# Decode step with modulation: the output projection's weights in one load, and the result turned through a bf16 PSUM tile

## The chip, the cores and the metric

The kernel runs on one core of one Trainium2 chip. Times are device microseconds (us) of whole executions, as medians of several runs. Profile times are microseconds from the start of the profiled execution's span, which is about 1.3 us shorter than its timed duration (420.02 against 418.7 us).

## The reference

One decode step of a modulated transformer block for two sequences: attention with 32 query heads over 4 key/value heads and 32768 cached positions, a projection `wo`, then a two-layer network. Cut to what matters here:

```python
mod = (silu(c) @ w_mod)                       # 6 vectors of 1024 for each sequence
h = layernorm(x) * (1 + ca) + sa
q = h @ wq                                    # 1024 -> 32 heads of 128
p = softmax(q @ k_cache.T * 128 ** -0.5)      # caches: 2 x 4 x 32768 x 128, bf16
o = p @ v_cache
x = x + ga * (o.reshape(B, 1, 4096) @ wo)     # wo: 4096 x 1024, 8 MB
h = layernorm(x) * (1 + cb) + sb
x = x + gb * (gelu(layernorm(h) @ w1 + b1) @ w2 + b2)   # w1, w2: 7.3 MB each
return x                                      # 2 x 1 x 1024, bf16
```

## The kernel before

All large inputs are streamed through a ring of 160 KB per partition. A list `stream` holds the loads in order; each has a place in the ring, and SyncE issues the next one when everything that had used that place has been read. The order of issue is fixed, so one load that has to wait holds up all behind it.

```python
def add_k(i, hf):   # K of round i in two halves of 32 KB to a partition
    add(("K", i, hf), [2, TPC * D], ..., hf * 32 * KB, f"K{hf}")      # places 0 and 32
def add_v(i):       # V of round i, 64 KB to a partition
    add(("V", i), [NCH, TPC * D], ..., 64 * KB, "V")                  # place 64
# ... w_mod, then wq (places 96 and 128), then K, K, V of the 8 rounds, then:
for m, off in enumerate((128, 0)):
    add(("wo", m), [16, DM], A_wo[m * 2048:(m + 1) * 2048, :].rearrange("(p j) n -> p j n", j=16), off * KB)
for m, off in enumerate((32, 64)):
    add(("w1", m), [4, F], w1_v[:, 4 * m:4 * m + 4, :], off * KB)
for m, (j0, j1, off) in enumerate(W2_ITEMS):  # 8, 8, 8, 3 and 1 rows of w2
    add(("w2", m), [j1 - j0, DM], w2_v[:, j0:j1, :], off * KB)
```

A round transposes K on the PE, multiplies it with q, takes the softmax and multiplies with V. At its end the head outputs are rescaled, picked out of a 128x128 product and put into `atT`, the transposed operand of the `wo` product:

```python
dve(... scalar_tensor_tensor(out=pick[:, :, :], in0=psM[:, 256:384] ..., scalar=rinv[:, 0:1], in1=m8 ...))
dve(... tensor_reduce(at[:, :], pick.rearrange("p e j -> p j e"), AX.X, ALU.add))
lo = 64 * (g % 2)
T.inst("pool", lambda e: e.tensor_copy(atT[g // 2][lo:lo + 64, :, b], at[lo:lo + 64, :]), ...)
```

After the rounds come the loads of two biases, the `wo` product (64 matmuls on four column groups of the PE), two layernorms, the `w1` product, gelu, the `w2` product (32 matmuls into rows for its first 16 rows, 96 into columns for the last 12), and the turn of the result:

```python
for m in range(2):
    it = need("wo", m)
    for j in range(16):
        for hf in range(2):
            q = 2 * (j % 2) + hf
            pe(... matmul(psS[0][32 * q:32 * q + 32, :], lhsT=atT[m][:, j, :], rhs=w[:, j, hf * 512:(hf + 1) * 512], ...))
# ... layernorm, w1, gelu, w2 ...
pe(... matmul(psM[0:16, 0:128], lhsT=res_bf.rearrange("p b k -> p (b k)"), rhs=ident[:, :], start=True, stop=True))
dve(lambda e: e.tensor_copy(res16[:, :], psM[0:16, 0:128]), ...)     # psM is float32
```

## Time and profile before

| | before |
|---|---|
| median, three runs | 420.02 us (419.86 to 420.03) |
| span of the profile | 418.7 us |
| bytes loaded, mean rate over the span | 178.42 MB, 426 GB/s |
| last bytes of the stream | before 415.5 us |
| PE, VectorE, ScalarE busy | 70%, 50%, 36% |

The profile is read from two sides. The busy rows show which resource never rests (the DMA engines). The timeline of the last 90 us shows each group of instructions with its start, its length and, in brackets, how long its engine had stood idle and what ended that. A group whose bracket names a DMA waited for bytes; a group whose bracket names an engine waited for computing. The lines themselves are in the prediction.

### The profile page before, as it was taken

The numbers are of one execution on the slowest core, as the hardware profiler recorded it, in microseconds if no ns is written. First come the engines' busy times: TensorE is split into PE (matmuls) and PEld (weight loads), VectorE is DVE, ScalarE is ACT, GpSimd is POOL, SyncE is SP. The second block draws the span as 40 slices with busy tenths as digits, with TensorE's granted clock in tenths as the row PEclk, the third lists the DMA queues.
The fourth block names the chain that finished last, engine by engine and source line by source line (L and its number), as shares of the span: only waits on it lengthen the run. The fifth ranks groups of instructions, "written<-read, shape, count | busy, mean of one in ns | idle before, by whom it ended". The sixth has DMA issues, their size and how long they took to land.

```text
span 418.7 us, 11609 instructions
## 1 busy us (share of the span) xinstructions
PE 291.0 (70%) x5183; PEld 231.3 (55%) x5183; DVE 209.6 (50%) x423; ACT 149.4 (36%) x179; POOL 6.8 (2%) x29
## 2 busy tenths in 40 slices
PE   1407449766996895699369957976995699564536
PEld 1104219762993794299149926962894399221214
DVE  1201105546677676467726664766477567620411
ACT  2000015533565364256405632643365166400100
POOL 3000000000000000000000000000000000000000
PEclk9999557986896997799589958986697889576585
DMA  9989999999999999999999999999999999899995
GB/s 373 450 380 449 448 404 493 398 406 446 441 432 429 423 451 429 419 454 457 391 435 476 407 416 448 438 438 426 438 438 426 416 460 457 377 448 428 424 427 249
DMA packets 5581, 178.42 MB, mean 426 GB/s; under 512 B 698, under 2 KB 706, under 8 KB 964
## 3 DMA queue, kind: packets, MB, share of 16 engines
q1 hardware_dynamic: 5572, 178.28, 98.8%
q8 instruction: 8, 0.13, 0.1%
q14 instruction: 1, 0.01, 0.0%
HBM read 178.28 MB, written 0.00 MB: 426 GB/s over the span
## 4 chain that ended last, share of the span: by engine, by line
DMA 71%; PE 24%; DVE 2%; issue 1%; ACT 1%; SPq 1%
DMA V<-in_A_v_cache_dram 39%; DMA wo<-in_A_wo_dram 10%; DMA K<-in_A_k_cache_dram 10%; PE psZ L584 10%; DMA w<-in_B_w_dram 9%; PE psKT L536 8%; DMA wmod<-in_w_mod_dram 4%; PE psS L548 1%; PE psZ L548 1%; PE psS L655 1%; PE psZ L729 1%; PE psZ L469 1%; ACT KT_sb L540 0%; PE psS L469 0%; DVE m1c L553 0%
## 5 line engine op out<-in xcount | busy, mean ns | idle before, releaser
L536 PE MATMUL psKT<-ident,K 128*128 128x128 bf16 x2048 | 163.1, 229 | 11.5 <-DMA K<-in_A_k_cache_dram 11.5
L540 ACT ACTIVATE KT_sb<-psKT 128x1024 bf16<-128x1024 bf16 x96 | 98.2, 1025 | 124.4 <-PE psKT L536 124.4
L542 DVE COPY KT_sb<-psKT 128x1024 bf16<-128x1024 bf16 x160 | 106.7, 688 | 61.6 <-PE psKT L536 61.2
L536 PEld LDWEIGHTS psKT<-ident,K 128*128 128x128 bf16 x2048 | 126.7, 102 | 13.0 <-DMA K<-in_A_k_cache_dram 12.7
L584 PE MATMUL psZ<-V,E_sb 128*32 128x512 bf16 x512 | 46.4, 541 | 23.2 <-DMA V<-in_A_v_cache_dram 20.0
L548 PE MATMUL psS<-qcur,KT_sb 128*128 128x8 bf16 x1024 | 44.7, 167 | 2.2 <-issue 2.2
L584 PEld LDWEIGHTS psZ<-V,E_sb 128*32 128x32 bf16 x512 | 18.7, 130 | 47.7 <-issue 38.8
L548 PE MATMUL psZ<-qcur,KT_sb 128*128 128x8 bf16 x1024 | 43.0, 167 | 2.2 <-issue 1.5
L548 PEld LDWEIGHTS psS<-qcur,KT_sb 128*128 128x128 bf16 x1024 | 40.0, 97 | 2.3 <-issue 2.3
L548 PEld LDWEIGHTS psZ<-qcur,KT_sb 128*128 128x128 bf16 x1024 | 37.9, 96 | 3.4 <-issue 1.6
L572 ACT ACTIVATE E_sb<-S_sb 128x512 bf16<-128x512 f32 x32 | 19.5, 630 | 29.6 <-DVE S_sb L570 29.6
L570 DVE TENSOR_TENSOR S_sb<-S_sb,gmb 128x512 f32<-128x512 f32 x32 | 20.0, 685 | 0.3
L576 DVE TENSOR_REDUCE rs<-E_sb 128x8 f32<-128x512 bf16 x32 | 19.7, 675 | 0.0
L469 PE MATMUL psS<-wmod,inT 128*32 128x512 bf16 x32 | 5.1, 624 | 16.2 <-DMA wmod<-in_w_mod_dram 16.2
L553 DVE TENSOR_REDUCE m1c<-psZ 128x8 f32<-128x512 f32 x16 | 11.1, 693 | 10.2 <-ACT S_sb L552 10.1
L595 DVE RECIPROCAL rinv<-psM 128x1 f32<-128x1 f32 x8 | 1.3, 168 | 27.7 <-PE psM L593 27.7
L605 PE MATMUL psM<-msum,hmat 128*128 128x128 f32 x16 | 4.2, 347 | 13.3 <-DVE msum L600 13.3
L559 PE MATMUL psM<-identf,m 128*8 128x128 f32 x16 | 4.3, 369 | 13.1 <-DVE m L556 13.1
L553 DVE TENSOR_REDUCE m1c<-psS 128x8 f32<-128x512 f32 x16 | 11.1, 693 | 3.2 <-ACT S_sb L552 3.1
L552 ACT ACTIVATE S_sb<-psZ 128x512 f32<-128x512 f32 x16 | 9.5, 595 | 7.5 <-PE psZ L548 7.5
L477 DVE COPY S_sb<-psS 128x512 f32<-128x512 f32 x1 | 0.7, 690 | 22.9 <-PE psS L469 22.9
L469 PEld LDWEIGHTS psS<-wmod,inT 128*32 128x32 bf16 x32 | 1.1, 132 | 19.3 <-DMA wmod<-in_w_mod_dram 18.0
(123 smaller groups left out, 167.5 us busy)
## 6 DMA issues: line engine op xcount, KB each, us to landing
K<-in_A_k_cache_dram SPq DMA_DIRECT2D x16, 4096.0 KB, 27.1
wq<-in_A_wq_dram SPq DMA_DIRECT2D x2, 4096.0 KB, 44.8
wo<-in_A_wo_dram SPq DMA_DIRECT2D x2, 4096.0 KB, 39.0
w<-in_B_w_dram SPq DMA_DIRECT2D x2, 3584.0 KB, 32.5
wmod<-in_w_mod_dram SPq DMA_DIRECT2D x1, 6144.0 KB, 29.8
w<-in_B_w_dram SPq DMA_DIRECT2D x3, 2048.0 KB, 37.8
wmod<-in_w_mod_dram SPq DMA_DIRECT2D x1, 4608.0 KB, 15.8
wmod<-in_w_mod_dram SPq DMA_DIRECT2D x1, 1536.0 KB, 6.0
```

Of the source, the lines that this page charges most:

```text
L469: pe(lambda e, w=it.view, k=k, kk=kk, ch=ch, n=n, q=q: e.matmul(bank[n][32 * q:32 * q + 32, :], lhsT=inT[:, k, :], rhs=w[:, kk, ch * 512:( ...
L536: pe(lambda e, kq=kq, jj=jj, w=kt, t=t: e.transpose(psKT[kq][:, jj * 128:(jj + 1) * 128], w[:, t, :], ident[:, :]), reads=[it.reg, "ident" ...
L540: act(lambda e, src=src: e.activation(KT_sb[g8][:, :, :], src, ACT.Copy), reads=[f"psKT{kq}"], writes=[f"KT_sb{g8}"], sem=f"ev{cc}_{g8}")
L542: dve(lambda e, src=src: e.tensor_copy(KT_sb[g8][:, :, :], src), reads=[f"psKT{kq}"], writes=[f"KT_sb{g8}"], sem=f"ev{cc}_{g8}")
L548: pe(lambda e, t=t, jj=jj: e.matmul(ps[:, t * HPG:(t + 1) * HPG], lhsT=KT_sb[g8][:, jj, :], rhs=qcur[:, :], start=True, stop=True), reads= ...
L552: act(lambda e: e.activation(Sc, ps.rearrange("p (t h) -> p h t", h=HPG), ACT.Copy), reads=[preg], writes=[f"S_sb_{cc}"], sem=f"sc{cc}")
L553: dve(lambda e: e.tensor_reduce(m1c[:, :, cc], ps.rearrange("p (t h) -> p h t", h=HPG), AX.X, ALU.max), reads=[preg], writes=[f"m1c{cc}"])
L559: pe(lambda e: e.matmul(psM[0:HPG, 0:128], lhsT=m1[:, :], rhs=identf[:, :], start=True, stop=True), reads=["m1", "identf"], writes=["psM"])
L570: dve(lambda e: e.tensor_tensor(Sc, Sc, gmb[:, :].unsqueeze(2).to_broadcast([128, HPG, TPC]), ALU.subtract), reads=[f"S_sb_{cc}", "gmb"], ...
L572: act(lambda e: e.activation(Ec, Sc.rearrange("p h (u t) -> p u h t", t=4), ACT.Exp, scale=SCALE), reads=[f"S_sb_{cc}"], writes=[f"E_sb_{c ...
L576: dve(lambda e: e.tensor_reduce(rs4[:, :, cc], Ec.rearrange("p u h t -> p h u t"), AX.XY, ALU.add), reads=[f"E_sb_{cc}"], writes=[f"rs4_{c ...
L584: pe(lambda e, t4=t4, tg=tg, q=q: e.matmul(psO[32 * q:32 * q + 32, :], lhsT=E_sb[:, tg // 4, :, :].rearrange("p h t -> p (h t)"), rhs=vt[: ...
```

## The change

Its intent: one 8 MB load of `wo`, with 64 contiguous KB to a partition, in place of two of 4 MB with 32 KB, which needs another row layout (a partition holds 32 consecutive rows, so each head group fills a quarter of the partitions and not a half of one of two operands); and a cheaper last step, in which the result is transposed into a bf16 PSUM tile and copied from there. The core of the diff (shapes of the small helpers `hmat`, `rsum16`, `m8`, `pick` change with it, cut here):

```diff
-W2_ITEMS = (..., (16, 24, 128), (24, 27, 144), (27, 28, 150))
+W2_ITEMS = (..., (16, 24, 0), (24, 27, 16), (27, 28, 22))
-    at = sb("at", [128, 16], BF16)
-    atT = [sb(f"atT{i}", [128, 16, 32], BF16) for i in range(G // 2)]
+    at = sb("at", [128, 32], BF16)
+    atT = sb("atT", [128, 32, 32], BF16)
-    for m, off in enumerate((128, 0)):
-        add(("wo", m), [16, DM], A_wo[m * 2048:(m + 1) * 2048, :].rearrange("(p j) n -> p j n", j=16), off * KB)
+    add(("wo", 0), [32, DM], A_wo.rearrange("(p j) n -> p j n", j=32), 0)
-    for m, off in enumerate((32, 64)):
+    for m, off in enumerate((128, 64)):
         add(("w1", m), ...)
-        lo = 64 * (g % 2)
-        ... e.tensor_copy(atT[g // 2][lo:lo + 64, :, b], at[lo:lo + 64, :]) ...
+        lo = 32 * g
+        ... e.tensor_copy(atT[lo:lo + 32, :, b], at[lo:lo + 32, :]) ...
-    for m in range(2):
-        it = need("wo", m)
-        for j in range(16):  ... lhsT=atT[m][:, j, :] ...
+    it = need("wo", 0)
+    for j in range(32):  ... lhsT=atT[:, j, :] ...
-    pe(lambda e: e.matmul(psM[0:16, 0:128], lhsT=res_bf..., rhs=ident[:, :], start=True, stop=True), ...)
-    dve(lambda e: e.tensor_copy(res16[:, :], psM[0:16, 0:128]), ...)
+    pe(lambda e: e.transpose(psKT[0][0:16, 0:128], res_bf..., ident[:, :]), ...)
+    dve(lambda e: e.tensor_copy(res16[:, :], psKT[0][0:16, 0:128]), ...)
```

More of the change, by code (lines that the diff above doesn't have):

```diff
@@ L36 @@
 WMOD_ITEMS = ((0, 1), (1, 4), (4, 8))
-W2_ITEMS = ((0, 8, 96), (8, 16, 112), (16, 24, 128), (24, 27, 144), (27, 28, 150))
+W2_ITEMS = ((0, 8, 96), (8, 16, 112), (16, 24, 0), (24, 27, 16), (27, 28, 22))
 EVAC_PATTERN = ("dve", "act", "dve", "act", "dve", "dve", "act", "dve")
@@ L258, in bass_adaLN_cond__gqa_block_cached__mixer_channel_mlp__decode_kernel @@
     onesf = sb("onesf", [128, 128])
-    hmat = sb("hmat", [128, 2, HPG, 8])
+    hmat = sb("hmat", [128, G, HPG, 4])
     hsel = sb("hsel", [128, HPG])
     mk4 = sb("mk4", [128, 4])
-    m8 = sb("m8", [128, 8])
+    m8 = sb("m8", [128, 4])
     mblk = sb("mblk", [128, KT8])
@@ L265, in bass_adaLN_cond__gqa_block_cached__mixer_channel_mlp__decode_kernel @@
     c16 = sb("c16", [16, 128], BF16)
-    rsum16 = sb("rsum16", [128, 2, HPG, 8])
+    rsum16 = sb("rsum16", [128, G, HPG, 4])
     msum = sb("msum", [128, 128])
@@ L411, in bass_adaLN_cond__gqa_block_cached__mixer_channel_mlp__decode_kernel @@
     T.inst("pool", lambda e: e.memset(onesf[:, :], 1.0), writes=["onesf"])
-    for t, nm in [(inT, "inT"), (gT, "gT")] + [(atT[g], f"atT{g}") for g in range(G // 2)]:
+    for t, nm in ((inT, "inT"), (gT, "gT"), (atT, "atT")):
         T.inst("pool", lambda e, t=t: e.memset(t[:, :, :], 0.0), writes=[nm])
@@ L451, in bass_adaLN_cond__gqa_block_cached__mixer_channel_mlp__decode_kernel @@
     dve(lambda e: e.tensor_reduce(hsel[:, :], identf.rearrange("p (c h t) -> p h c t", c=4, h=HPG), AX.XY, ALU.add), reads=["identf"], writes=["hsel"])
-    dve(lambda e: e.tensor_copy(hmat[:, :, :, :], hsel[:, :].unsqueeze(1).unsqueeze(3).to_broadcast([128, 2, HPG, 8])), reads=["hsel"], writes=["hmat"])
-    dve(lambda e: e.tensor_reduce(m8[:, :], identf.rearrange("p (h e) -> p e h", e=8), AX.X, ALU.add), reads=["identf"], writes=["m8"])
+    dve(lambda e: e.tensor_copy(hmat[:, :, :, :], hsel[:, :].unsqueeze(1).unsqueeze(3).to_broadcast([128, G, HPG, 4])), reads=["hsel"], writes=["hmat"])
+    dve(lambda e: e.tensor_reduce(m8[:, :], identf.rearrange("p (h e) -> p e h", e=4), AX.X, ALU.add), reads=["identf"], writes=["m8"])
     dve(lambda e: e.tensor_reduce(mblk[:, :], identf.rearrange("p (k u) -> p k u", u=16), AX.X, ALU.add), reads=["identf"], writes=["mblk"])
@@ L527, in next_q @@
         b, g = i % 2, i // 2
-        T.inst("pool", lambda e: e.tensor_copy(qcur[:, :], qT[:, b, g * HPG:(g + 1) * HPG]), reads=["qT"] + [f"atT{g}" for g in range(G // 2)], writes=["qcur"], sem="qc")
+        T.inst("pool", lambda e: e.tensor_copy(qcur[:, :], qT[:, b, g * HPG:(g + 1) * HPG]), reads=["qT", "atT"], writes=["qcur"], sem="qc")
     def tr(i, cc, g8):
@@ L591, in row_sums @@
         dve(lambda e: e.tensor_reduce(rowsum[:, :], rs4[:, :, :], AX.X, ALU.add), reads=[f"rs4_{cc}" for cc in range(NCH)], writes=["rowsum"])
-        dve(lambda e: e.tensor_copy(rsum16[:, :, :, :], rowsum[:, :].unsqueeze(1).unsqueeze(3).to_broadcast([128, 2, HPG, 8])), reads=["rowsum"], writes=["rsum16"], sem="rs")
+        dve(lambda e: e.tensor_copy(rsum16[:, :, :, :], rowsum[:, :].unsqueeze(1).unsqueeze(3).to_broadcast([128, G, HPG, 4])), reads=["rowsum"], writes=["rsum16"], sem="rs")
         pe(lambda e: e.matmul(psM[:, 144:145], lhsT=rsum16.rearrange("p g h e -> p (g h e)"), rhs=onesf[:, 0:1], start=True, stop=True),
@@ L606, in extract_2 @@
            reads=["hmat", "msum"], writes=["psM"])
-        dve(lambda e: e.scalar_tensor_tensor(out=pick[:, :, :], in0=psM[:, 256:384].rearrange("p (e j) -> p e j", j=16), scalar=rinv[:, 0:1],
-                                             in1=m8[:, :].unsqueeze(2).to_broadcast([128, 8, 16]), op0=ALU.mult, op1=ALU.mult),
+        dve(lambda e: e.scalar_tensor_tensor(out=pick.rearrange("p e j -> p (e j)").rearrange("p (e j) -> p e j", j=32), in0=psM[:, 256:384].rearrange("p (e j) -> p e j", j=32), scalar=rinv[:, 0:1],
+                                             in1=m8[:, :].unsqueeze(2).to_broadcast([128, 4, 32]), op0=ALU.mult, op1=ALU.mult),
             reads=["psM", "rinv", "m8"], writes=["pick"], sem="pk")
@@ L612, in red @@
             with nc.allow_low_precision("one nonzero term in each sum"):
-                return e.tensor_reduce(at[:, :], pick.rearrange("p e j -> p j e"), AX.X, ALU.add)
+                return e.tensor_reduce(at[:, :], pick.rearrange("p e j -> p (e j)").rearrange("p (e j) -> p j e", j=32), AX.X, ALU.add)
         dve(red, reads=["pick"], writes=["at"])
-        lo = 64 * (g % 2)
-        T.inst("pool", lambda e: e.tensor_copy(atT[g // 2][lo:lo + 64, :, b], at[lo:lo + 64, :]), reads=["at"], writes=[f"atT{g // 2}"], sem="ac")
+        lo = 32 * g
+        T.inst("pool", lambda e: e.tensor_copy(atT[lo:lo + 32, :, b], at[lo:lo + 32, :]), reads=["at"], writes=["atT"], sem="ac")
     rounds = {}
@@ L648, in bass_adaLN_cond__gqa_block_cached__mixer_channel_mlp__decode_kernel @@
     T.dma("sp", lambda e: e.dma_start(b1m[:, :], B_b1.rearrange("(q r) -> q r", r=448)), key="ld_b1", writes=["b1m"])
-    for m in range(2):
-        it = need("wo", m)
-        for j in range(16):
-            for hf in range(2):
-                q = 2 * (j % 2) + hf
-                pe(lambda e, w=it.view, m=m, j=j, hf=hf, q=q: e.matmul(psS[0][32 * q:32 * q + 32, :], lhsT=atT[m][:, j, :], rhs=w[:, j, hf * 512:(hf + 1) * 512],
-                                                                       start=(m == 0 and j < 2), stop=(m == 1 and j >= 14), skip_group_check=True),
-                   reads=[it.reg, f"atT{m}"], writes=["psS0"], mark=(j == 15 and hf == 1))
+    it = need("wo", 0)
+    for j in range(32):
+        for hf in range(2):
+            q = 2 * (j % 2) + hf
+            pe(lambda e, w=it.view, j=j, hf=hf, q=q: e.matmul(psS[0][32 * q:32 * q + 32, :], lhsT=atT[:, j, :], rhs=w[:, j, hf * 512:(hf + 1) * 512],
+                                                              start=(j < 2), stop=(j >= 30), skip_group_check=True),
+               reads=[it.reg, "atT"], writes=["psS0"], mark=(j == 31 and hf == 1))
     def load_row(e_name, b, b_reg, n, parts=128):
@@ L733, in bass_adaLN_cond__gqa_block_cached__mixer_channel_mlp__decode_kernel @@
     dve(lambda e: e.tensor_tensor(res_bf.rearrange("p b k -> p k b"), mT[:, :, :], x1b[:, :, :], ALU.add), reads=["mT", "x1b"], writes=["res_bf"])
-    pe(lambda e: e.matmul(psM[0:16, 0:128], lhsT=res_bf.rearrange("p b k -> p (b k)"), rhs=ident[:, :], start=True, stop=True),
-       reads=["res_bf", "ident"], writes=["psM"])
-    dve(lambda e: e.tensor_copy(res16[:, :], psM[0:16, 0:128]), reads=["psM"], writes=["res16", "c16"])
+    pe(lambda e: e.transpose(psKT[0][0:16, 0:128], res_bf.rearrange("p b k -> p (b k)"), ident[:, :]), reads=["res_bf", "ident"], writes=["psKT0"])
+    dve(lambda e: e.tensor_copy(res16[:, :], psKT[0][0:16, 0:128]), reads=["psKT0"], writes=["res16", "c16"])
     s_out = nc.alloc_semaphore("s_out")
```

## The prediction

> **What bounds the kernel now.** I read the page first: the slices and the chain that ended last.
>
> ```profile
> DMA  9989999999999999999999999999999999899995
> DMA 71%; PE 24%; DVE 2%; issue 1%; ACT 1%; SPq 1%
> ```
>
> The DMA engines are busy from the first slice to the last but one; no compute engine is. The page adds 178.42 MB at a mean of 426 GB/s: 178.42 / 0.426 = 419 us, the whole span (418.7 us). So the kernel is one stream of loads, and a change counts only if it (a) opens a hole in the stream, (b) changes its rate or bytes, or (c) moves the few microseconds after the last load. Next I read the timeline of the last 90 us, where everything the diff touches lies, apart from small work in each round.
>
> ```profile
> 330.98 14.05 SPq L389 DMA_DIRECT2D wo<-in_A_wo_dram  x2
> 355.02 21.65 SPq L389 DMA_DIRECT2D w<-in_B_w_dram  x7
> 362.51 6.34 PE L584 MATMUL psZ<-V,E_sb 128*32 128x512 bf16 x64 [2.93 <-DMA V<-in_A_v_cache_dram]
> 372.10 3.25 PE L655 MATMUL psS<-wo,atT 128*32 128x512 bf16 x32 [0.78 <-DMA wo<-in_A_wo_dram]
> 381.73 3.55 PE L655 MATMUL psS<-wo,atT 128*32 128x512 bf16 x32 [6.39 <-DMA wo<-in_A_wo_dram]
> 385.34 0.69 DVE L664 COPY S_sb<-psS 128x512 f32<-128x512 f32 x1 [13.23 <-PE psS L655]
> 395.75 1.68 PE L696 MATMUL psZ<-w,inT 128*32 128x448 bf16 x16
> 400.59 1.12 DVE L704 STREAM_TRANSPOSE S_sb<-psZ 128x896 f32<-128x896 f32 x1 [2.84 <-PE psZ L696]
> 403.68 1.05 PE L720 MATMUL psS<-w,gT 128*32 128x512 bf16 x16 [3.15 <-DMA w<-in_B_w_dram]
> 408.41 1.90 PE L720 MATMUL psS<-w,gT 128*32 128x512 bf16 x16 [3.69 <-DMA w<-in_B_w_dram]
> 413.27 2.91 PE L729 MATMUL psZ<-gT,w 128*128 128x2 bf16 x96 [0.30 <-DMA w<-in_B_w_dram]
> 417.03 0.28 DVE L736 CAST c<-psM 16x128 bf16<-16x128 f32 x1 [0.37 <-PE psM L734]
> ```
>
> The bracket gives the idle time before a group and what ended it. The last V lands at about 362.4, the first half of wo at about 371.9, the second at 381.65, w1's second half by 398.7, and pieces of w2 at 403.6, 408.4 and 413.2: arrivals set the pace, and the PE waits for each. From wo to w2 there are thus spare microseconds between "computed" and "landed". The first fetch of w, at 355.02, comes when the last K half has been transposed, which frees its buffer; the same moment will release the new wo.
>
> The stretches between landings give the rate (columns: stretch, its length, busy time of the five engines, granted clock, DMA share, GB/s):
>
> ```profile
> 343.00:362.40 19.40, 14.23 (x331) 13.40 (x328) 13.88 (x26) 10.62 (x15) 0.00 (x0) 0.88 0.97 421
> 362.40:371.90 9.50, 7.14 (x68) 3.16 (x68) 4.67 (x13) 1.86 (x2) 0.00 (x0) 0.68 1.02 442
> 371.90:381.65 9.75, 3.25 (x32) 1.09 (x32) 0.20 (x1) 0.00 (x0) 0.25 (x1) 0.68 0.97 420
> ```
>
> The first stretch is (nearly) the last V: 8.39 MB, and 64 KB to a partition, in 19.4 us. The other two are wo, 4.19 MB each and 32 KB to a partition: 9.50 + 9.75 = 19.25 us for the same bytes. The rate depends little, if at all, on whether a partition gets 32 or 64 KB.
>
> **What the Trainium skill says.** (1) "DMA: Bandwidth & Descriptors", Where 436 GB/s comes from: 16 ports of 32 bytes at 850 MHz give 435.2 GB/s. The trace agrees: 434 GB/s over the stretch from 60 to 320 us, 426 over the span. Nothing is left to win in the rate. (2) Same page, Queues, rings and completion order: each DMA engine takes its descriptors in ring order. So wo, issued behind V, starts when V is through, however early it was issued; that agrees with wo landing 41.1 us after its issue at 330.98. (3) "TensorE: Matmul & The Clock Gate", Part 1: the PE starts at half clock and gets the full one after some 3.4 us of activity, in free-running windows. The trace agrees: the second 32 wo matmuls take 3.55 us (111 ns each), with a granted clock of 0.50 from 381.5 to 385.0 and 1.00 from 385.5; w1's last 32 take about 1.8 us (56 ns each). (4) "VectorE: DVE Perf Modes", Why PSUM operands drop a tier: a source in PSUM allows at most the two-fold mode, and float32 there none. The trace agrees: a bf16 PSUM copy of 128x1024 takes 688 ns, a float32 one of 128x512 takes 690 ns.
>
> **The change part by part.**
>
> *One load of 8 MB in place of two of 4.* Same bytes, same place in the queue. One issue less (0.35 us on the SyncE queue, which is not on the path). The old halves were issued at 330.98 (its space was free) and 344.7 (first K half transposed). The new one covers the space of both K halves, so it goes out at 355.02. At that moment the queue still holds the rest of V: 362.4 - 355.0 = 7.4 us of work for the average engine. Is that enough? A hole needs an engine to run dry before the first wo descriptor reaches it. The engines' spread at the end of the stream is an upper guess of their skew: the last microseconds run 352, 246, 197, 86, 0 GB/s in half microseconds from 413.5, so the fastest engine ends some 2 to 2.5 us ahead of the slowest. 7.4 - 2.5 = 4.9 us are left for an issue to reach the engines; the whole out-store, issue to landing, takes 1.4 us. So: no hole, cost 0. wo then lands at 381.7, as its second half does now.
>
> *The order behind it.* w1's first half moves to space free since wq, so its only wait is the queue's order: it follows wo at 355.4 (now 355.02). The second half and the first two pieces of w2 still wait for the last V's matmuls (368.8). The last three w2 pieces wait for the wo matmuls, now over at 375.4, then at about 388. At 388 there is still queued work until w2's second piece lands at 408.4: 20 us. Cost 0.
>
> *The wo matmuls.* Now 32 run at 372.1 under the second half's load, and 32 after 381.7. Afterwards all 64 run after 381.7: the first 32 cold, 3.5 us; the other 32 warm at 56 ns, 1.8 us, or cold, 3.5 us. So the row copy (385.34) and everything that hangs on it is 1.8 to 3.5 us later. Follow that. inT is ready for w1 at 395.75 + 1.8..3.5 = 397.6..399.3. The 64 w1 matmuls took 4.8 us, of which part was a wait for the second half, landed at 398.7. Now they are limited by the PE: at most 38 cold (107 ns) and 26 warm (56 ns) = 5.5 us, so they end at 402.9 to 404.8 instead of 400.55. From there to gT it was 402.74 - 400.55 = 2.2 us: 405.1 to 407.0. The 16 matmuls of w2's first piece (landed 403.6) take 1.05 warm or 1.9 cold: done at 406.2 to 408.6. The second piece lands at 408.4. So the delay ends in the wait for it: cost 0, at the worst corner about 0.2 us, and that meets the 0.3 us between the end of the column turn (412.98) and the landing at 413.2. The spare time, 3.7 us before the second piece, is what pays for it.
>
> *A possible gift.* With the PE working later, its idle gap before 408.4 shrinks from 3.7 us to 0-2 us, so it may still be warm for the end. The 96 last matmuls take 2.91 us at clock 0.50. Warm, they could save up to 0.5 us, no more, since the last piece itself lands only at about 415.4 and 8 matmuls follow. I give that 30%: -0.15 us on average.
>
> *The turn of the result.* The product with the identity into float32 PSUM becomes a transpose into bf16 PSUM: 276 ns as before by my estimate (same 128 columns). The copy reads bf16: by the two rows above, a column costs 690-688 = about the same for twice the columns, so 128 columns fall from 133 to 67 ns above the same 150: 0.28 to 0.21 us. On the path: -0.07 us. Its bank was last used in the rounds, so there is no new wait.
>
> *In each of the 8 rounds.* The pick works on 4 x 32 instead of 8 x 16: still 128 elements, 0.35 + 0.37 us, and a 32x32 GpSimd copy for a 64x16 (0.25 us). All come after the signal that releases the next V load (the row sums' matmul, L593) and before a K transposition that waits for its load. Cost 0.
>
> Sum: 420.02 - 0.07 - 0.15 + about 0.1 for the corners = 419.9 us.
>
> **Rivals.** *A hole in the stream.* The new wo waits for the last transposition, and the queue is down to 7.4 us, less than in any round (14 us of K were still to land when the last V was issued at 329.08). For it: with a late issue an engine that runs far ahead would idle, and DMA idle time is lost for good. Against it: the spread of about 2.5 us. If true, 1 to 5 us: 421 to 425. *The tail becomes compute-bound.* Nothing of wo is worked off before 381.7; if all of it ran cold and w1 too, w2's first piece would be done a microsecond after the second landed. Against it: 3.7 us spare. It would make 420.3 to 421.5. *A gain from fewer, larger packets.* For it: one completion less. Against it: V with 64 KB (421 GB/s) isn't faster than wo with 32 KB (430). If true by 2% over 8 MB, 0.4 us: 419.6. *A loss of rate from 64 KB to a partition:* the same size, the other way: 420.4.
>
> **Range and chances.** The sum is 419.9; a stream of 178 MB repeats within about 0.1 us here (419.86 to 420.03), but another order of loads can land some tenths apart. 8 in 10: 419.2 to 420.9, wider above, for the hole. Two per cent are 8.4 us: no term above comes near, up or down. Faster 0.01, same 0.98, slower 0.01.
>
> **What would show it.** Right: one wo issue at about 355, the DMA busy as before between 350 and 365, the first wo matmul at about 381.7, 64 of them in 5.3 to 7 us, the row copy at 387 to 389, the PE waiting for the second w2 piece at about 408.4 and for the third at 413.2, a last copy of about 0.21 us. Wrong: a dip in DMA share near 358 to 363 and every later landing shifted by it (the hole); no wait before the second w2 piece's matmuls (compute-bound); all landings shifted from wo on without a dip (rate).

## The result, and the profile after

The changed kernel takes 419.93 us (median of six runs, 419.79 to 420.10), the kernel before 420.01 us (six runs, 419.86 to 420.07). The ratio is 0.9999, with a 95% interval from 0.9986 to 1.0011: the same time. Ratios here are the mean time of one kernel's runs over the mean of the other's in the same rounds, so not quite the ratio of the medians quoted. The one above takes in all six runs; those of the experiments leave out each kernel's first run, the profiled one, which the medians and ranges include.

The page of the changed kernel, the row of the DMA engines and the chain that ended last:

```profile
DMA  9989999999999999999899999999999999999996
DMA 73%; PE 26%; SPq 0%; issue 0%; DVE 0%
```

The stream is as full as before. (Line by line the chain now runs through K, 56%, where it ran through V, 39%: wo's issue now hangs on the last K transposition, so the walk back takes that branch. It is another path through the same full stream, not another time.) The timeline of the changed kernel, SyncE's issues first, then the groups that answer to those shown of before:

```profile
353.55 0.35 SPq L388 DMA_DIRECT2D wo<-in_A_wo_dram  x1
353.94 35.77 SPq L388 DMA_DIRECT2D w<-in_B_w_dram  x7
...
362.57 5.21 PE L583 MATMUL psZ<-V,E_sb 128*32 128x512 bf16 x64 [4.46 <-DMA V<-in_A_v_cache_dram]
381.79 5.83 PE L653 MATMUL psS<-wo,atT 128*32 128x512 bf16 x64 [11.54 <-DMA wo<-in_A_wo_dram]
387.68 0.69 DVE L662 COPY S_sb<-psS 128x512 f32<-128x512 f32 x1 [16.64 <-PE psS L653]
398.29 1.68 PE L694 MATMUL psZ<-w,inT 128*32 128x448 bf16 x16
404.15 1.12 DVE L702 STREAM_TRANSPOSE S_sb<-psZ 128x896 f32<-128x896 f32 x1 [3.85 <-PE psZ L694]
406.35 1.55 PE L718 MATMUL psS<-w,gT 128*32 128x512 bf16 x16 [2.27 <-DVE gT L709]
408.46 1.87 PE L718 MATMUL psS<-w,gT 128*32 128x512 bf16 x16 [0.56 <-DMA w<-in_B_w_dram]
413.48 2.84 PE L727 MATMUL psZ<-gT,w 128*128 128x2 bf16 x96 [1.29 <-DMA w<-in_B_w_dram]
417.17 0.21 DVE L733 COPY c<-psKT 16x128 bf16<-16x128 bf16 x1 [0.36 <-PE psKT L732]
```

Three things are to be seen. First, wo goes out 22.6 us later than its first half did (353.55 against 330.98), and its matmuls still start at 381.79, where the second half's started at 381.73. Second, the row copy is 2.3 us later (387.68 against 385.34), w2's first matmuls 2.7 us later (406.35 against 403.68), and the group after that starts within 0.05 us of where it did (408.46 against 408.41): the bracket before it has shrunk from 3.69 to 0.56 us. What was lost came out of a wait. Third, the last copy takes 0.21 us in place of 0.28.

So the times agree because the stream sets the end, and the changed parts either keep their place in the stream or lie in waits for it. Two parts of this can be tried: how much later wo's issue could still be, and how much later the work behind wo.

### The profile page after: what moved, and what is told of

Read it like the earlier page. It is cut to its first block, busy times and chain, and to the rows that moved or that the text cites. A ratio compares the mean times of both kernels' runs of the same rounds, so it can differ in the third digit from the quotient of the medians.

```text
span 418.8 us, 11607 instructions
## 1 busy us (share of the span) xinstructions
PE 284.7 (68%) x5183; PEld 226.4 (54%) x5183; DVE 209.6 (50%) x423; ACT 149.3 (36%) x179; POOL 7.3 (2%) x28
## 4 chain that ended last, share of the span: by engine, by line
DMA 73%; PE 26%; SPq 0%; issue 0%; DVE 0%
DMA K<-in_A_k_cache_dram 56%; PE psKT L535 18%; DMA wo<-in_A_wo_dram 7%; DMA w<-in_B_w_dram 6%; DMA wmod<-in_w_mod_dram 4%; PE psS L547 3%; PE psZ L547 2%; PE psS L653 1%; PE psZ L727 1%; PE psZ L468 1%; PE psS L468 0%; SPq L388 0%; SPq L403 0%; SPq L404 0%; PE psKT L732 0%
## 5 line engine op out<-in xcount | busy, mean ns | idle before, releaser
L535 PE MATMUL psKT<-ident,K 128*128 128x128 bf16 x2048 | 159.8, 226 | 13.2 <-DMA K<-in_A_k_cache_dram 13.2
L535 PEld LDWEIGHTS psKT<-ident,K 128*128 128x128 bf16 x2048 | 123.9, 101 | 14.6 <-DMA K<-in_A_k_cache_dram 14.6
L583 PE MATMUL psZ<-V,E_sb 128*32 128x512 bf16 x512 | 44.8, 526 | 27.0 <-DMA V<-in_A_v_cache_dram 25.4
L653 PE MATMUL psS<-wo,atT 128*32 128x512 bf16 x64 | 5.8, 545 | 11.5 <-DMA wo<-in_A_wo_dram 11.5
```

Of the source, the lines that this page charges most:

```text
L535: pe(lambda e, kq=kq, jj=jj, w=kt, t=t: e.transpose(psKT[kq][:, jj * 128:(jj + 1) * 128], w[:, t, :], ident[:, :]), reads=[it.reg, "ident" ...
L583: pe(lambda e, t4=t4, tg=tg, q=q: e.matmul(psO[32 * q:32 * q + 32, :], lhsT=E_sb[:, tg // 4, :, :].rearrange("p h t -> p (h t)"), rhs=vt[: ...
L653: pe(lambda e, w=it.view, j=j, hf=hf, q=q: e.matmul(psS[0][32 * q:32 * q + 32, :], lhsT=atT[:, j, :], rhs=w[:, j, hf * 512:(hf + 1) * 512] ...
```

## The experiments

Each is an edit of the changed kernel unless it says otherwise; each gave correct results. "Landing" below is taken from the start of the matmuls that waited for the load.

### wo_in_v: wo issued after the last V has been used

```diff
-    add(("wo", 0), [32, DM], ..., 0)
+    add(("wo", 0), [32, DM], ..., 64 * KB)
-    for m, off in enumerate((128, 64)):
+    for m, off in enumerate((128, 0)):
-W2_ITEMS = ((0, 8, 96), (8, 16, 112), (16, 24, 0), (24, 27, 16), (27, 28, 22))
+W2_ITEMS = ((0, 8, 28), (8, 16, 44), (16, 24, 64), (24, 27, 80), (27, 28, 86))
```

> The changed kernel with wo put into the space of V instead of that of the two K halves, so that its load can only be issued after the last V's matmuls (about 368, some 6 us after the last V has landed at 362.5); the other pieces of w1 and w2 go to space that is free earlier. Theory (the kernel is one stream of loads, and the change cost nothing because at the issue of wo, 353.6, 9 us of V were still queued): the stream runs dry, wo and every landing after it come later by 368.1 - 362.4 plus an issue-to-first-data time of 1.5 to 2 us, 7 to 8 us in all: about 427.5 us (426.5 to 428.5). Rival (the late issue of wo doesn't matter, because the end is set by the chain of compute after wo, which has spare time to lose): less than 4 us, under 424.

Measured: 429.48 us (429.07 to 430.62) against 420.19, ratio 1.0232 (1.0215 to 1.0249). The timeline, then the stretches around the hole (columns as in the prediction: length, busy time of the five engines, clock, DMA share, GB/s):

```profile
367.54 0.35 SPq L388 DMA_DIRECT2D wo<-in_A_wo_dram  x1
389.67 5.14 PE L653 MATMUL psS<-wo,atT 128*32 128x512 bf16 x64 [19.71 <-DMA wo<-in_A_wo_dram]
417.42 1.90 PE L718 MATMUL psS<-w,gT 128*32 128x512 bf16 x16 [2.72 <-DMA w<-in_B_w_dram]
```

```profile
357.50:360.00 2.50, 0.41 (x2) 0.31 (x2) 2.02 (x5) 1.13 (x2) 0.00 (x0) 0.50 0.97 419
360.00:362.50 2.50, 0.17 (x4) 0.17 (x8) 2.50 (x6) 2.48 (x4) 0.00 (x0) 0.50 0.02 4
```

The hole is there (the DMA share is 0.02 from 360.0 to 362.5), and it is paid in full, so the rival falls: spare time in the chain behind wo buys nothing for a stream that has run dry. wo lands 7.9 us later than in the changed kernel (389.67 against 381.79), as expected. But the time grew by 9.3 us, over the expected 7 to 8: from wo's landing to that of w2's second piece it took 27.75 us, against 26.67 in the changed kernel. This further 1.1 us was not expected; the next runs meet it again, and wo_wait_m1 shows where it arises.

A remark on reading: the stretch shows almost no bytes after 360.0, yet V's matmuls are released at 362.33. A load is moved in packets, and the kept trace lists each with its start and length. A packet of V or wo has 64 KB and takes 2.42 us; V's last ones start before 360.0 and end between 360.3 and 361.9. So the view books a packet's bytes when it starts. The first packets of wo start 1.0 to 1.8 us after its issue (368.5 to 369.3); the expectation's 1.5 to 2 us for this had no measurement behind it. And these first 16 packets, one on each engine, take 2.6 to 3.4 us in place of 2.42.

### wo_wait_max and wo_wait_m1: wo issued closer to the landing of the last V

```diff
+    T.wait("sp", reads=["gmb"])      # wo_wait_max; reads=["m1"] in wo_wait_m1
     it = need("wo", 0)
```

> The changed kernel, with one more wait before wo's issue: the SyncE queue waits for the last round's broadcast maximum, so wo goes out at about 358.3 instead of 353.6, with 4 us of V still queued for the average engine. Theory (a hole needs an engine to run dry; skew 2 to 2.5 us by the prediction's estimate, issue to first data 1.5 to 2 us): 4.1 - 2.5 - 2 is about zero: 419.9 to 420.5 us, every landing after wo at most 0.5 us later. Rival (the margin of the changed kernel is already nearly used up, the skew is larger): 1.5 to 4 us more, 421.5 to 424.

Measured: 422.08 us (420.92 to 422.40) against 420.19, ratio 1.0038 (1.0021 to 1.0054). The rounds of this profiled run were later on the PE, so wo went out at 360.95 and not at 358.3; the planned dose was missed.

```profile
360.95 0.35 SPq L388 DMA_DIRECT2D wo<-in_A_wo_dram  x1
...
362.83 5.67 PE L583 MATMUL psZ<-V,E_sb 128*32 128x512 bf16 x64 [2.12 <-DMA V<-in_A_v_cache_dram]
382.95 5.85 PE L654 MATMUL psS<-wo,atT 128*32 128x512 bf16 x64 [11.98 <-DMA wo<-in_A_wo_dram]
410.91 1.90 PE L719 MATMUL psS<-w,gT 128*32 128x512 bf16 x16 [1.81 <-DMA w<-in_B_w_dram]
```

wo lands 1.2 us later than in the changed kernel and w2's second piece 2.5 us later: as after the large hole, a further loss arises behind wo (27.96 us between the two, against 26.67). All 16 first packets of wo are slow here too, 2.6 to 3.5 us. The loss of 2.2 us lies in the rival's range, but at a later issue than either side was stated for. The earlier wait was a second dose:

> A second dose of the margin, as the first came out smaller than planned (wo_wait_max issued wo only 1.9 us before the last V landed, and lost 2.2 us). Here the SyncE queue waits for the last round's first maximum, some 2 us earlier: wo goes out about 4 to 6 us before the last V lands at 362.5. Theory (data of a load start 1.0 us after its issue, as in the two runs with a hole, and the engines finish V within 2.4 us of each other, one packet of 64 KB): no engine runs dry, 419.9 to 420.3 us. Rival (the stream needs wo queued long before): over 420.8.

Measured: 421.33 us, scattered from 420.01 to 421.97, against 420.08, ratio 1.0019 (1.0004 to 1.0035). In the profiled run, of 421.97 us:

```profile
358.62 0.35 SPq L388 DMA_DIRECT2D wo<-in_A_wo_dram  x1
...
382.34 5.75 PE L654 MATMUL psS<-wo,atT 128*32 128x512 bf16 x64 [11.94 <-DMA wo<-in_A_wo_dram]
410.49 1.90 PE L719 MATMUL psS<-w,gT 128*32 128x512 bf16 x16 [2.52 <-DMA w<-in_B_w_dram]
```

The expectation was wrong: 3.9 us before V's landing (362.51) is not enough, though one of the four runs lost nothing. Only 0.55 us was lost up to wo; another 1.5 us by w2's second piece (28.15 us from wo's landing, against 26.67). The median of the four, 421.33, is where its rival put it, over 420.8. The end of the stream shows where the loss is: in the last three microseconds with traffic, 415 to 418, it moves 117, 25 and 10 GB/s, where the changed kernel moves 221 and 64 from 414 to 416 and nothing more. 25 GB/s is about what one of 16 engines carries (434 / 16 = 27). So one engine finishes late, and a load counts as landed only with its last engine.

The packets in the trace say how. Five of the 16 first packets of wo take longer than the usual 2.42 us, 2.53 to 3.49 us, and one engine had stood idle for at least 0.6 us before its first. The slowest packet, of 3.49 us, starts at 361.55; followed from packet to packet, its engine ends wo at 381.97, the others by 381.37. At 388.33, six packets of w1 later, one engine moves a packet of 16 KB for another queue, of which the page shows only the sum:

```profile
q8 instruction: 8, 0.13, 0.1%
```

That packet takes 0.93 us, and the w1 packet next to it 1.56 in place of 1.06: 1.4 us in all. The trace doesn't name engines, but the sum says that it is the late one: 381.97 + 16 packets of w1 at 1.06 + 1.41 = 400.34, where w1's second half in fact ends (the other engines by 398.57). w2's second piece then ends at 410.06, on the others by 408.29.

An instruction packet at this place stands in every kept trace, in the changed kernel at 388.41. There the engines end wo at 379.9 to 381.4, and the one that carries this packet is among the first, at 379.93: its lead of 1.5 us hides the 1.4 us. After a late issue of wo the lead is gone and the packet shows. In wo_in_v, where all engines start wo within 0.8 us of each other, the engine with this packet ends 0.9 us behind the rest, most of the further 1.1 us. What remained was why a late issue takes the lead away: why the first packets are slow, and what the small loads in front of wo have to do with it.

### m1_biases_early and finest_biases_early: the small bias loads out of the way

Between the last V and wo lie five loads of biases, 9.0 KB in all (the expectations' 7.9 is a slip: 2 KB of b2 and 7 KB of b1), on 1 to 8 partitions. The Trainium skill, "DMA: Bandwidth & Descriptors", Why a DMA increments its semaphore by 16 and not by 1, says that a load over few partitions runs on as few engines, the lowest-numbered ones. The trace has one packet for each row, 16 in all; no run here shows an engine's number.

```diff
 # against wo_wait_m1; finest_biases_early: the same against w2_finest, without the wait
+    # at the kernel's start, from ScalarE's queue:
+    for r0, r1 in ((0, 1), (1, 3), (3, 7), (7, 8)):
+        T.dma("act", ... b2m[r0:r1, :] ...)
+    T.dma("act", ... b1m ...)
     ...
-    # the same five from SyncE's queue, before wo
```

> wo_wait_m1 with the five small loads of the two biases (7.9 KB in all, a few hundred bytes to a packet) taken from between the last V and wo and issued from ScalarE's queue at the kernel's start. wo_wait_m1 lost 0.0 to 2.0 us although wo was issued 3.9 us ahead of the last V's landing; its stream ends in a taper, 117, 25, 10 GB/s in the last three microseconds, the rate of one engine alone, so one or a few engines lag behind the rest. Theory A (the small loads run one after the other on the few lowest engines, with nothing queued behind them when wo is late, so these engines start wo late; the page on DMA says that few partitions mean few engines): without them the loss is gone, 419.8 to 420.2 us, and no taper. Theory B (the late issue of wo itself makes engines lag): as wo_wait_m1, 420 to 422 us with the same scatter.

Measured: 419.99 us (six runs: four from 419.87 to 420.07, two of 421.52 and 422.76) against 419.98, ratio 1.0018 (0.9997 to 1.0039). Inconclusive. Two runs still lost over a microsecond, so the bias loads are not the whole cause, if any of it. The four good runs can't be credited to them either: in the profiled one wo went out at 357.45, 4.9 us ahead of V's landing (362.33), and not 3.9. In that run no first packet of wo is slow, and the stream ends as in the changed kernel. Against theory A speak the packets of wo_wait_m1: the bias loads take 0.02 or 0.04 us each, 0.5 us in all, far too little for a lag of over a microsecond. For theory B (the late issue itself) speak the slow first packets of wo after each of the later issues. Why they are slow stays open, and so does what the engines did in the runs without a profile.

> w2_finest with the small bias loads at the start likewise: the candidate for a version faster than both kernels. In the changed kernel, too, the stream tapers off: 221 and 64 GB/s in the last two microseconds. Theory A: part of that taper is the lag that the small loads give the lowest engines before wo; without it the last pieces land 0.3 to 1 us earlier, and with pieces this small the end follows them: 419.2 to 419.7 us. Theory B (the taper is the engines' ordinary spread): 419.9 to 420.1.

Measured (w2_finest, below, with the bias loads at the start): 419.90 us (419.78 to 420.32) against 419.98, ratio 0.9995 (0.9982 to 1.0007). Not distinguishable from either kernel; in its profile, of the slowest run, the taper is 270 and 102 GB/s, no shorter than w2_finest's 229 and 80. Theory B fits better.

### w1_ahead: the hole of wo_in_v filled with w1

As wo_in_v, with w1's first half, whose place is free, issued before wo:

```diff
-    add(("wo", 0), [32, DM], ..., 64 * KB)
     for m, off in enumerate((128, 0)):
         add(("w1", m), [4, F], ..., off * KB)
+        if m == 0:
+            add(("wo", 0), [32, DM], ..., 64 * KB)
```

> As wo_in_v, but with w1's first half, whose space is free, issued ahead of wo, so that it fills the hole: the stream's bytes come without a gap and end at about 415.4 as in the changed kernel, while wo lands 8.7 us later (about 390.4). Theory (the chain of compute from wo's landing to gT takes 24.6 us, 381.8 to 406.4, and is PE-bound from there): gT at 415, then the 32 products of w2's first two pieces, the turn, the 96 last products: end at about 422 to 424 where the changed kernel has 416.3, so 426 to 427.5 us, though the stream has no hole. Rival (only the stream counts): 420 to 421.

Measured: 426.96 us, widely scattered (425.13 to 429.32), against 420.08, ratio 1.0183 (1.0155 to 1.0210). In the profiled run, of 425.13 us:

```profile
390.15 5.37 PE L654 MATMUL psS<-wo,atT 128*32 128x512 bf16 x64 [19.66 <-DMA wo<-in_A_wo_dram]
...
413.81 3.29 PE L719 MATMUL psS<-w,gT 128*32 128x512 bf16 x32 [2.27 <-DVE gT L710]
418.81 2.56 PE L728 MATMUL psZ<-gT,w 128*128 128x2 bf16 x96
```

From wo's landing to w2's matmuls it is 23.7 us (24.6 in the changed kernel), and neither of the last two groups waited for a DMA: the end is bound by computing, 5.3 us behind the changed kernel's (418.81 against 413.48), in a stream without a hole. So both limits are real: the stream must not run dry, and wo must land early enough for the chain behind it. The scatter was not expected. In this run wo was issued at 368.06, and the packets of the w1 half before it end between 369.1 and 370.5, so the lead was only 1.0 to 2.4 us. Almost no engine stood idle (0.2 us over all 16), yet the ten packets of wo that start first, from 369.0 to 369.9, take 2.55 to 3.47 us, and the six from 370.2 on the usual 2.42. So after an issue this late the first packets are slow even where hardly any engine ran dry. The slower runs of this kernel have no profile; why they are slower is not shown.

### after_plus4 and before_plus4: the same extra work behind wo in both kernels

```diff
+        if j == 31:                      # before_plus4: the last j of the second half
+            for _ in range(19):
+                pe(... matmul(psM[:, :], lhsT=ident[:, :], rhs=w[:, 0, 0:512], start=True, stop=True), mark=False)
```

> The changed kernel with 19 idle products (128x512, into a PSUM bank that nobody reads) before the last wo product: the row copy comes about 4 us later (387.7 to 391.7). Theory (the compute chain behind wo has spare time that the change used up in part: of it 0.56 us before w2's second piece and 1.29 us before w2's third are left): gT at 410.3, past the landing of the second piece at 408.4, then PE-bound to the end: the time is 4 - 0.56 - 1.29 = about 2.1 us more, 422 us (420.6 to 422.8, as the clock falls). Rival (the stream alone sets the end, whatever the chain does): no change, under 420.4. Rival (the chain is on the path already): the full 4 us, 424.

> The kernel before with the same 19 idle products before its last wo product. Theory: gT moves from 402.7 to 406.8, the matmuls of w2's first piece end by 408.7, and the second piece lands at 408.4: nothing or up to 0.3 us is lost: 420.0 to 420.4. So the two kernels, equal in time, differ by about 2 us under the same load. Rival (both have the same spare time, as they have the same time): the same rise as in the changed kernel.

Measured: the changed kernel 421.63 us (421.18 to 422.33), ratio 1.0045 (1.0029 to 1.0060); the kernel before 420.03 us (419.92 to 420.04, and one of 421.36), ratio 1.0012 (0.9996 to 1.0027); both against 419.96. First the changed kernel, then the one before, each with the extra work:

```profile
409.57 3.52 PE L722 MATMUL psS<-w,gT 128*32 128x512 bf16 x32 [2.27 <-DVE gT L713]
...
414.81 2.60 PE L731 MATMUL psZ<-gT,w 128*128 128x2 bf16 x96
```

```profile
408.03 1.91 PE L724 MATMUL psS<-w,gT 128*32 128x512 bf16 x32 [2.27 <-DVE gT L715]
...
413.20 2.88 PE L733 MATMUL psZ<-gT,w 128*128 128x2 bf16 x96 [1.40 <-DMA w<-in_B_w_dram]
```

In the kernel before, the last products still wait 1.40 us for w2: the extra work, which moved the row copy by 5.3 us there (385.34 to 390.63), fitted in. In the changed kernel it moved the row copy by 4.1 us (387.68 to 391.79), the wait is gone, and the last products start 1.3 us later (414.81 against 413.48). w2's first products start 1.5 us later there than in the kernel before (409.57 against 408.03), although its extra work was 1.2 us shorter: the 2.7 us between them is what the change had moved at this place (406.35 against 403.68). That supports the prediction's account of where wo's later matmuls went.

The 1.3 us lost at the end has a rival in it: the PE's clock. The 32 products of w2's first two pieces ran at half clock in the changed kernel (3.52 us) and at full clock in the one before (1.91 us). Without these 1.6 us the last products could have started at 413.2, about when their bytes landed. So the pair shows that the changed kernel has less spare time; that 1.3 us of it is all due to the spent reserve is not shown.

### wo_two_loads: the new layout in two loads

```diff
-    add(("wo", 0), [32, DM], A_wo.rearrange("(p j) n -> p j n", j=32), 0)
+    for m in range(2):
+        add(("wo", m), [16, DM], A_wo.rearrange("(p j) n -> p j n", j=32)[:, 16 * m:16 * m + 16, :], 32 * m * KB)
 # the loop of the wo matmuls, which now waits for each half in turn, is cut here
```

> The changed kernel, with its row layout of 32 rows to a partition, but loaded as two halves of 32 KB to a partition, the first going out when the first K half is transposed. Theory (rate is the same with 32 and 64 KB to a partition, and a later wo product has spare time): 419.9 us as the changed kernel, within 0.3; wo lands at the same 381.7, the first half at about 372, and the row copy comes back to about 385.3 from 387.7, with no gain at the end. Rival (64 KB to a partition is slower or faster by 2%): wo's second half lands 0.4 us earlier or later than in the changed kernel.

Measured: 420.10 us (420.03 to 420.15) against 420.19, ratio 1.0000 (0.9983 to 1.0017).

```profile
381.62 3.19 PE L654 MATMUL psS<-wo,atT 128*32 128x512 bf16 x32 [5.77 <-DMA wo<-in_A_wo_dram]
...
408.29 1.90 PE L719 MATMUL psS<-w,gT 128*32 128x512 bf16 x16 [3.34 <-DMA w<-in_B_w_dram]
```

The second half lands at 381.62, 0.17 us from the single load, so a packet of 32 or 64 KB makes no difference that could be seen here (in the trace one takes 1.21, the other 2.42 us). The wait before w2's second piece is back (3.34 us) without any gain in time: earlier work behind wo is worth nothing as it is, but it leaves the larger reserve.

### turn_only: the turn of the result alone, in the kernel before

The edit is the last hunk of the diff above.

> The kernel before with only the turn of the result changed (transpose into bf16 PSUM and a bf16 copy). Theory: the copy takes 0.21 instead of 0.28 us, the PE instruction the same 0.27 to 0.28; the time is 0.07 us less, which the rounds cannot resolve: 419.95, ratio 0.9985 to 1.0015. Rival (the transpose brings a wait for its bank or for the PE's mode): a gap over 0.1 us before the transpose or the copy.

Measured: 419.97 us (419.93 to 420.08) against 420.19, ratio 0.9997 (0.9981 to 1.0014).

```profile
416.72 0.28 PE L734 MATMUL psKT<-ident,res_bf 128*16 128x128 bf16 x1 [0.53 <-DVE res_bf L733]
417.03 0.21 DVE L735 COPY c<-psKT 16x128 bf16<-16x128 bf16 x1 [0.37 <-PE psKT L734]
```

The bracket before the transpose is what it was (0.53 us), so no wait came with it, and the copy is 0.07 us shorter. It lies on the path, so the saving should be real, but the rounds can't resolve it.

### w2_finer and w2_finest: smaller last pieces of w2

The last products run without a stop after w2's third piece has landed; if they were the limit, an earlier part of that piece should help.

```diff
-W2_ITEMS = (..., (16, 24, 0), (24, 27, 16), (27, 28, 22))
+W2_ITEMS = (..., (16, 20, 0), (20, 24, 8), (24, 27, 16), (27, 28, 22))                            # w2_finer
+W2_ITEMS = (..., (16, 20, 0), (20, 24, 8), (24, 26, 16), (26, 27, 20), (27, 28, 22))              # w2_finest
```

> The changed kernel with w2's third piece (8 rows, landing at 413.4, 64 of the 96 last products waiting for it) cut into two of 4 rows. Theory: in the changed kernel the last 96 products run without a stop from 413.48 to 416.32, 0.9 us past the end of the load stream (415.4); with half a piece earlier (about 411) 32 of them are done before, and the end is the last landing plus some products: 0.3 to 0.6 us less, 419.4 us (ratio about 0.999). Rival (one more completion, or smaller packets, cost the stream as much as is won): no difference, or slower.

> The changed kernel with w2's last 12 rows in pieces of 4, 4, 2, 1, 1 in place of 8, 3, 1. w2_finer showed that the end is set by the landing of the 3-row piece (415.15) and the 32 products behind it (1.0 us), not by the first 64. Theory: with 2, 1, 1 rows the 3-row piece's first 16 products go at about 414.6, and only 8 to 16 are left behind the last landing: end of the products at about 415.8 to 416.0 in place of 416.3, 0.3 to 0.5 us less, 419.5 us, at the edge of what the rounds resolve; the spans show it (418.2 to 418.4 in place of 418.6). Rival (the last landing itself is later with more pieces, or close behind the 3-row piece's): no gain.

Measured: w2_finer 420.00 us (419.94 to 420.11) against 419.96, ratio 1.0001 (0.9987 to 1.0015); w2_finest 420.02 us (419.94 to 420.17) against 420.08, ratio 0.9999 (0.9985 to 1.0013). The last groups of w2_finer, then of w2_finest:

```profile
412.82 1.84 PE L727 MATMUL psZ<-gT,w 128*128 128x2 bf16 x64
415.17 1.01 PE L727 MATMUL psZ<-gT,w 128*128 128x2 bf16 x32 [0.50 <-DMA w<-in_B_w_dram]
```

```profile
415.98 0.38 PE L727 MATMUL psZ<-gT,w 128*128 128x2 bf16 x8 [0.22 <-DMA w<-in_B_w_dram]
```

Both theories failed and their rivals held. The products did start earlier, and then waited again: in w2_finer the last 32 for the piece of 3 rows, which lands at about 415.15, in w2_finest only the last 8 for the very last row, at about 415.9. In the changed kernel the products end at 413.48 + 2.84 = 416.32, in w2_finer at 416.18, in w2_finest at 415.98 + 0.38 = 416.36. These lie together, so taking one limit away only shows the other. No version beats the two kernels.

## Why the prediction was right

- *The stream sets the end; the rate doesn't depend on 32 or 64 KB to a partition.* Right: wo landed at 381.79 (predicted 381.7), and within 0.17 us of that in two loads.
- *No hole at the late issue of wo.* Right for the changed kernel, but its margin was overstated. The prediction left 4.9 us in reserve after the engines' spread. The doses, by how long before the last V's landing wo went out, each from one profiled run: 9.0 us (the changed kernel) and 7.5 us (w2_finest, 355.16) cost nothing; 4.9 us (m1_biases_early) nothing; 3.9 us cost 1.9 us (421.97 against 420.08); 1.9 us cost 2.2 (422.40 against 420.19); 5.2 us too late cost 8.9 (429.07 against 420.19). So of the 9 us some 4 to 5 were needed, more than the spread of the engines alone, which is 1.6 us at the end of V (360.5 to 362.1) and not 2 to 2.5. What the prediction left out: after a late issue wo's first packets are slow (up to 3.5 us in place of 2.42), and without its lead the engine that carries the instruction packet ends up to 1.4 us behind the others. Why those first packets are slow is open.
- *The wo matmuls take 5.3 to 7 us, the delay ends in the wait for w2's second piece.* Right: 5.83 us, the row copy at 387.68, a wait of 0.56 us left. The two runs with extra work agree with it, with the reservation about the clock made there.
- *w2's first piece done at 406.2 to 408.6, so at most 0.2 us lost.* The last corner is a slip: 407.0 + 1.9 = 408.9, so 0.5 us. Measured were 406.35 + 1.55 = 407.9, and the slip didn't matter.
- *The w1 product at most 5.5 us.* A little too short: 5.8 us (398.29 to 404.1), since the PE stayed at half clock until about 403.3, longer than assumed. The slack took it.
- *A gift of up to 0.5 us from a warm PE, at 30%.* It did not come: the clock fell back to half at 413.6, as the last products began (2.84 us). And its size was overstated: after_plus4, warm for most of them, ran the 96 in 2.60 us. The closeness of the sum (419.9 against 419.93) is in part luck: the gift of 0.15 us and the 0.1 us for the corners nearly cancel, and neither came.
- *The turn: 0.07 us.* Right: 0.213 against 0.278 us, with the PE instruction unchanged (0.27 to 0.28 us).
- *The rounds: nothing.* Right: the reduction to 32 columns takes 368 ns against 366, and GpSimd's copy of 32x32 takes 316 ns against 249 for 64x16, off the path.

## What to carry to other kernels

In a kernel that is one stream of loads, ask of every edit only whether it changes the bytes, opens a hole, or moves the work behind the last landings; a later product is free as long as a wait for bytes follows it, and a later issue as long as enough is still queued in front of it. But two kernels of equal time need not be equally safe: read the idle time before each group that waits for a load, and the lead of each issue over the moment the queue runs empty, as the reserve that the next change can use. Here the change spent 3.1 of 3.7 us of the one and left 7.5 to 9 us of the other (as the profiled builds show), of which some 4 to 5 were needed.

## What the Trainium skill lacked or had wrong

- "DMA: Bandwidth & Descriptors", Rules for kernel authors, says to issue a load early but not by how much to lead a running stream. Here 9.0 and 7.5 us of queued work were enough, 4.9 us was in the run profiled, 3.9 us was not (1.9 us lost, in a run where wo itself landed only 0.55 us late).
- The same page, Latency and other measured facts, gives about 0.6 us to the first byte for loads issued from SyncE, but not from when it counts. In wo_in_v, on an idle queue, the first packet of wo starts 0.98 us after the start of the issuing instruction, which lasts 0.35 us, so 0.63 us after its end: it agrees if counted from there. The last of the 16 engines starts 0.8 us after the first.
- "TensorE: Matmul & The Clock Gate", Part 1, puts the rise of the clock at around 4 us of sustained work, give or take 0.5. That is too narrow here: the PE worked from 397.1 on and had half clock until 403.3, 6.2 us; in the kernel before, V's matmuls ran from 362.5 until 368.0, 5.5 us. The free-running windows of about 3.4 us in the same part do fit: the changed kernel's clock changes at 386.3, 389.7, 403.3, 406.8, 410.2 and 413.6, close to whole multiples of 3.41 us apart, and 399.9 to 403.3 is the first such window that the PE worked through without an idle stretch.
- No page read says how long a packet takes soon after a late issue (2.42 us is usual here for 64 KB; some that started 1.0 to 2.9 us after the issue took up to 3.5), or what a packet of instructions costs the engine of a running stream (16 KB: 1.4 us, on one of 16 engines).
